# Block products in a mixture-of-experts kernel: reordering the engines' queues, loading w_out a group earlier, and feeding the sums between half-steps

## The chip, the cores and the metric

One core of one Trainium2 chip. The metric is the device time of one execution in microseconds (us), the median over runs. The profile shows one execution. TensorE is called PE here, its weight loads PEld, VectorE DVE, ScalarE ACT, GpSimd POOL, and SyncE, which issues most DMAs, SP. Every engine works through its own queue in the order in which the built program has it.

## The reference

Three stages run one after the other on 2304 tokens of 512 values: random-feature attention, a gated feed-forward layer, and a layer of 8 experts with room for 288 tokens each.

```
x = attention(q, k, v, omega)                   # [2304, 512]
xn = x / rms(x) * rms_g
h = silu(xn @ w_gate) * (xn @ w_val)            # [2304, 1536]
y = h @ w_out
logits = y @ moe2_w_gate                        # [2304, 8]; greedy assignment, highest logit first
out[mask_e] = relu(y[mask_e] @ w1[e]) @ w2[e]   # for each expert e
```

The change touches only how `h` and the sums for it are scheduled, and the end of the attention stage before it.

## The kernel before, in words

Every float32 product is made of three products of a rounded "high" part and a "low" remainder, so each operand appears twice: a high copy (on ACT) and a low difference (on DVE or POOL). A product of two 128-row steps is therefore six matmuls (`product`).

The tokens form five blocks of 512, 512, 256, 512 and 512 columns. **Attention** runs in 81 ticks (`run_tick`), one item of work each, with up to five older items still in flight. Into these ticks go *half-steps* of the feed-forward layer for the first three blocks (`ffn_step_pe` and `ffn_step_el`: one half of `h` for 128 of the 1536 features, gate or value, twelve matmuls, then tanh on ACT, two products on DVE, the split of `h`, and its write to DRAM, `h_dr`), and *units* (`conv_pe`, `conv_el`), which unscramble 48 pieces of weights from 64-bit words: one ACT operation and three DVE operations each (lines 591 to 593). `PACE` is the number of units started per tick, `STEP` the number of half-steps per tick.

The last two blocks, LEFT and RIGHT, are not multiplied one by one. They are treated as one 2 by 2 block product that is done with seven products instead of eight (Winograd's form of Strassen). For this the **sums stage** forms four sums of x (`sum_1` to `sum_4`, from the sum `sum_left` of the high and low parts of LEFT, and a split copy of half of RIGHT, `r2`), each in two column halves. While DVE, ACT and POOL do that, PE finishes the half-steps of the small 256-column block that are left over.

Then come twelve **groups** (`group(f)`, f from 0 to 11, and a short thirteenth), one for each 128 features. In the program's order PE does in a group: the product `pa` (in bank gv), a `late` logit (below), the product `pe` (also a gv bank), the logits of LEFT of the group before, a product added to bank `bb`, one added to `pa`, the logits of RIGHT, a product added to `bb`, one to `bc`, one to `bd`. Between them stand: `copy(bb, pa)` and `copy(p5, pe)` on ACT; `bc = bb + p5` on DVE, which has to be done before PE may add to `bb` again; `copy(bd, bb)` on ACT; the gates (`gate` is tanh on ACT, `times_gate` and `times_value` are DVE), and the split of h (`keep_high` on ACT, `keep_low` on DVE with the DMA to `h_dr`). A group also prepares work for others: `turn_w(f, part)` makes the sums of the weights (part 0 on POOL two groups ahead, parts 1 and 2 on DVE, parts 3 and 4 the split into `ta` on ACT and POOL); `wo_split` loads two 128-row pieces of w_out, makes the high copy on ACT and leaves the low parts to `wo_part` on DVE; `lates_lg` and `lates_split` load, split, write back and multiply with the gate weights the twelve pieces of h of the first block ("late", tile xh on ACT and POOL); `ffn_rank_el` compares logits of two 128-token chunks per call (`ranks`, part on DVE, part on `st["eng"]`).

In the groups PE, DVE, ACT and POOL keep the written order (`manual_schedule`); in the sums stage and in attention only PE does, and a scheduler places the rest. After the groups, w_out's product (`ffn2`, 648 matmuls) is used as filler while DVE sorts the tokens to the experts (`route`), and the experts follow.

Of the kernel before, what the change touches and what calls it, by code (L numbers as in the profile page):

```python
# [51 lines left out]
STEP = 1.08  # L52
PACE = (0.5, 0.7, 0.65)
# [241 lines left out]
def kernel(ctx, tc, qT, kT, kC, v1, vC, om, wgv, rms, wo, woT, wg2, w1, w2, cfd, trd, out, dbg=None):  # L295
# [443 lines left out]
    st["eng"] = st["sub"] = nc.gpsimd  # L739
    st["rank"] = lambda: psL.tile([128, BLK // 128, 2 * E], F32, name="lg")  # L740

    def ffn_rank_el():
        for c0 in rks:
            ranks(nc, st["eng"], fp, cf[:, C_T:C_N].rearrange("p (a b) -> p a b", b=E), L, R, c0, 2)
        rks.clear()

    def ffn_step_pe():
        if not ready or ready[0][1:] not in gvs or (fq and fq[0][1] not in wogs):
            return False
        j, f, v = ready.pop(0)  # L750
        pg = ffn_pe(j, f, v)
        if (f, v) == (KF - 1, 1):
            del xblk[j]
        ffn_rank()
        if v and fq:
            ffn_lg(*fq.pop(0))
        fst["el"] = (j, f, v, pg)
        return True
# [78 lines left out]
    def run_tick(tick):  # L837
# [6 lines left out]
        ffn_step_pe()  # L844
# [17 lines left out]
        if tick >= FFN_AT:  # L862
            conv["step"] += STEP - 1
            if conv["step"] >= 1:
                conv["step"] -= 1
                ffn_step_pe()
                ffn_step_el()
# [27 lines left out]
    def wo_part():  # L895
# [17 lines left out]
    st["late"] = 0  # L913
# [8 lines left out]
    def late_split(f):  # L922
        hs = lates[f]
        nc.scalar.copy(hs[:, :, 0], hs.bitcast(F32)[:, :, 1])
        nc.gpsimd.tensor_sub(hs[:, :, 1], hs.bitcast(F32)[:, :, 1], hs[:, :, 0])  # L925
        nc.sync.dma_start(h_dr[:BLK // HB2, :, f].rearrange("b p x -> p b x"),
                          hs.bitcast(F32).rearrange("p b l t -> p b (l t)"))

# [5 lines left out]
    def sum_tile(name):  # L934
        pool, kw = (xp, dict(name="xl")) if name == "s3" else (sp, dict(name=name))
        t = pool.tile([128, 2, 2, BLK], F32R, **kw)
        sums[name] = t
        return t

    def sum_split(name, half, t, eng):  # L940
        s_ = slice(half * HF, half * HF + HF)
        o = sums[name] if name in sums else sum_tile(name)
        nc.scalar.copy(o[:, 0, :, s_], t)
        eng.tensor_sub(o[:, 1, :, s_], t, o[:, 0, :, s_])

    lf = {}

    def sum_left(half):
        s_ = slice(half * HF, half * HF + HF)
        lf[half] = stage.tile([128, KD, HF], F32, name="ws")  # L950
        nc.vector.tensor_add(lf[half], xlh[:, :, s_], xll[:, :, s_])
# [4 lines left out]
    s1, s2 = {}, {}  # L956

    def sum_1(half):
        s_ = slice(half * HF, half * HF + HF)
        s1[half] = temp()  # L960
        nc.vector.tensor_add(s1[half], xr[:, :2, s_], xr[:, 2:, s_])
        sum_split("s1", half, s1[half], nc.vector)

    def sum_2(half):
        nc.vector.tensor_sub(s1[half], s1[half], lf[half][:, :2])
        sum_split("s2", half, s1[half], nc.vector)

    def sum_3(half):
        s_ = slice(half * HF, half * HF + HF)
        t = temp()  # L970
        nc.vector.tensor_sub(t, lf[half][:, :2], xr[:, :2, s_])
        sum_split("s3", half, t, nc.gpsimd)

    def sum_4(half):
        nc.vector.tensor_sub(s1[half], lf[half][:, 2:], s1[half])
        sum_split("s4", half, s1[half], nc.vector)
        s_ = slice(half * HF, half * HF + HF)
        sum_split("r2", half, xr[:, 2:, s_], nc.gpsimd)

    def turn_w(f, part):  # L980

        b, t = wf.get(f), wf.get(("t", f))
        if part == 0:
            w = wsl[f]
            wf[f] = stage.tile([128, 4, HF], F32, name="ws")
            for h in (slice(0, 2), slice(2, 4)):
                nc.gpsimd.tensor_add(wf[f][:, h], w[:, 0].rearrange("p (b x) -> p b x", b=4)[:, h],  # L987
                                     w[:, 1].rearrange("p (b x) -> p b x", b=4)[:, h])
# [6 lines left out]
        else:  # L995
            i = part - 3
            o = ta[f, i] = sp.tile([128, 2, 2, HF], F32R, name="ta", bufs=3)
            nc.scalar.copy(o[:, 0], t[i])  # L998
            nc.gpsimd.tensor_sub(o[:, 1], t[i], o[:, 0])  # L999
# [42 lines left out]
    def group(f):  # L1042

        nxt = f + 1 if f + 1 < KF else None
        if f < KF:
# [11 lines left out]
        if f < KF:  # L1057
# [6 lines left out]
        if f < KF:  # L1064
            pe = wide(psG, "gv")
            product(pe, *t1, *both("s1"), True)
        if f:
            keep_low(RIGHT, f - 1, th2, hp2)
        if f == KF:
            return  # L1070
        p5 = wide(sp, "p5", bufs=2)
        nc.scalar.copy(p5, pe)
        if nxt:
            turn_w(nxt, 1)
            turn_w(nxt, 3)
# [16 lines left out]
        nc.scalar.copy(bd, bb)  # L1092
        nc.vector.tensor_add(p5, bb, p5)
        if nxt:
            turn_w(nxt, 4)
        if f + 2 < KF:
            turn_w(f + 2, 0)
        product(bc_, *b22, *both("s4"), False)
        ffn_rank()
        st["rank"] = lambda: psS.tile([128, 512], F32, name="late")[:, :BLK // 128 * 2 * E].rearrange(  # L1100
            "p (c e) -> p c e", e=2 * E)
# [14 lines left out]
    def lates_lg():  # L1116
        n = st["late"]
        if 0 < n <= KF:
            ffn_lg(0, n - 1, lates[n - 1])
            if n == KF:  # L1120
                st["late"] += 1
        if 0 < n < KF - 1:
            late_load(n + 1)

    def lates_split():
        if st["late"] < KF:
            late_split(st["late"])
            st["late"] += 1

    with tc.manual_schedule(engines={mybir.EngineType.PE}):  # L1130
        ins = iter([lambda: sum_left(0), lambda: sum_1(0), lambda: sum_1(1), lambda: sum_left(1),
                    lambda: turn_w(0, 0), lambda: sum_2(0), lambda: sum_2(1), lambda: sum_3(0), lambda: sum_3(1),
                    lambda: sum_4(0), lambda: sum_4(1), lambda: turn_w(0, 1), lambda: turn_w(0, 2),
                    lambda: turn_w(0, 3), lambda: turn_w(0, 4), lambda: turn_w(1, 0)])
        while ready:
            assert ffn_step_pe()
            ffn_step_el()
            for _ in range(2):
                next(ins, int)()
        for make in ins:  # L1140
            make()
        late_load(0)
        late_load(1)
        while fq:
            ffn_lg(*fq.pop(0))
        for t in (bb, bc_, bd):
            nc.tensor.matmul(t, xlh[:, 0, :128], xlh[:, 0], start=True, stop=True)
    with tc.manual_schedule(engines=in_order | {mybir.EngineType.Pool}):
# [332 lines left out]
```

## Time and profile before

| what | us |
|---|---|
| median of 3 runs (lowest, highest) | 935.31 (934.28, 936.63) |
| the profiled execution's own time | 935.55 |
| its span, first to last instruction | 933.8 |
| PE busy in the span | 887.0 (95%) |
| attention with half-steps and units, up to | 334 |
| sums stage | 334 to 361 |
| first matmul of groups 0, 1, 2, 3 | 361.00, 372.47, 386.27, 397.23 |
| first matmul of the w_out product, after the groups | 518.81 |

The span and the 1.75 us around it make the time of the profiled execution. Busy time of PE counts overlapping matmuls as modelled, so that the time between the starts of two matmuls is the better measure of its pace.

### The profile page before, as it was taken

The numbers are of one execution on the slowest core, as the hardware profiler recorded it, in microseconds if no ns is written. First come the engines' busy times: TensorE is split into PE (matmuls) and PEld (weight loads), VectorE is DVE, ScalarE is ACT, GpSimd is POOL, SyncE is SP. The second block draws the span as 40 slices with busy tenths as digits, with TensorE's granted clock in tenths as the row PEclk, the third lists the DMA queues.
The fourth block names the chain that finished last, engine by engine and source line by source line (L and its number), as shares of the span: only waits on it lengthen the run. The fifth ranks groups of instructions, "written<-read, shape, count | busy, mean of one in ns | idle before, by whom it ended". The sixth has DMA issues, their size and how long they took to land.

```text
span 933.8 us, 15697 instructions
## 1 busy us (share of the span) xinstructions
PE 887.0 (95%) x5780; PEld 764.2 (82%) x5780; DVE 624.8 (67%) x1392; ACT 412.3 (44%) x913; POOL 264.1 (28%) x317
## 2 busy tenths in 40 slices
PE   9999999999999978988889899999999999999996
PEld 8788888888889976656657677777779999999996
DVE  4899876566659996665677667777664655566652
ACT  5886665445446643444444201001004544454541
POOL 1364423223323366555543000000011222222211
PEclk9999999999999999999999999999999999999999
DMA  8656436443355424554535987777732566755651
GB/s 289 203 152 205 148 101 181 134 144 113 128 180 188 148 77 127 190 193 158 188 119 188 247 229 206 226 208 212 210 94 86 180 193 194 215 183 187 190 178 32
DMA packets 114110, 159.26 MB, mean 171 GB/s; under 512 B 6641, under 2 KB 71665, under 8 KB 114033
## 3 DMA queue, kind: packets, MB, share of 16 engines
q1 hardware_dynamic: 108224, 143.96, 49.7%
q0 software_dynamic: 3072, 9.44, 3.5%
q10 hardware_dynamic: 2736, 4.85, 1.4%
q8 instruction: 45, 0.74, 0.3%
q14 instruction: 33, 0.26, 0.1%
HBM read 114.19 MB, written 44.04 MB: 169 GB/s over the span
## 4 chain that ended last, share of the span: by engine, by line
PE 39%; issue 10%; DVE 10%; POOL 5%; ACT 2%; DMA 2%; SPq 0%; POOLq 0%; ACTq 0%; DVEq 0%
PE py L1225 15%; PE ph L1337 3%; PE ph L1340 3%; PE ph L1338 3%; PE py L1350 3%; PE py L1348 3%; PE py L1349 3%; DVE hp L1025 1%; DMA ws<-wo_dr 1%; POOL ws L987 1%; POOL xh L925 1%; POOL ta L999 1%; POOL out_dram L1384 1%; PE gv L1320 1%; PE po L1354 1%
## 5 line engine op out<-in xcount | busy, mean ns | idle before, releaser
L1225 PE MATMUL py<-wc,ht 128*128 128x512 f32 x624 | 160.2, 405 | 0.4 <-DMA ht<-h_dr 0.4
L1225 PEld LDWEIGHTS py<-wc,ht 128*128 128x128 f32 x624 | 112.6, 191 | 20.1 <-DMA ht<-h_dr 0.5
L675 PE MATMUL gv<-xh,wc 128*128 128x512 f32 (+1 forms) x288 | 105.5, 377 | 4.5 <-DVE th L688 3.3
L1196 DVE TENSOR_TENSOR wc<-ws,wc 128x512 fp32r<-128x512 f32 x128 | 84.6, 685 | 35.5 <-ACT wc L1206 35.5
L676 PE MATMUL gv<-xh,wc 128*128 128x512 f32 (+1 forms) x288 | 100.0, 358 | 0.0
L408 ACT ACTIVATE ft<-pp,mx 128x128 f32<-128x128 f32 x288 | 83.0, 375 | 27.6 <-DVE mx L405 27.2
L1350 PE MATMUL py<-ehh,wc 128*128 128x288 f32 x256 | 76.2, 298 | 0.0
L1348 PE MATMUL py<-ehh,wc 128*128 128x288 f32 x256 | 75.8, 296 | 0.0
L1349 PE MATMUL py<-ehl,wc 128*128 128x288 f32 x256 | 75.6, 295 | 0.0
L1337 PE MATMUL ph<-exh,wc 128*128 128x288 f32 x256 | 71.2, 300 | 0.0
L1236 ACT COPY ys<-py 128x512 f32<-128x512 f32 x18 | 10.6, 588 | 134.8 <-PE py L1225 126.9
L1338 PE MATMUL ph<-exh,wc 128*128 128x288 f32 x256 | 69.8, 296 | 0.0
L1206 ACT CAST wc<-ws 128x1024 fp32r<-128x1024 f32 x64 | 67.3, 1052 | 2.7 <-ACT ys L1236 2.7
L678 PE MATMUL gv<-xl,wc 128*128 128x512 f32 (+1 forms) x288 | 67.5, 356 | 0.0
L675 PEld LDWEIGHTS gv<-xh,wc 128*128 128x128 f32 x288 | 54.7, 190 | 12.6 <-DVE th L688 4.6
L1342 DVE SCALAR_TENSOR_TENSOR ehl<-ph,ehh 128x288 fp32r<-128x288 f32 x64 | 29.3, 458 | 46.6 <-ACT ehh L1341 43.2
L676 PEld LDWEIGHTS gv<-xh,wc 128*128 128x128 f32 x288 | 54.9, 191 | 6.5
L405 DVE TENSOR_REDUCE mx<-pp 128x4 f32<-128x512 f32 (+1 forms) x76 | 50.0, 658 | 15.1 <-PE pp L401 9.1
L678 PEld LDWEIGHTS gv<-xl,wc 128*128 128x128 f32 x288 | 49.7, 191 | 8.2
L1276 POOL DMA_INDIRECT xh<-y_dr,idc x3 | 3.1, 1040 | 171.4 <-DVE idc L1288 170.8
L999 POOL TENSOR_TENSOR ta<-dw,ta 128x512 fp32r<-128x512 f32 x24 | 31.6, 1318 | 66.6 <-ACT ta L998 66.4
L1384 POOL DMA_INDIRECT out_dram<-yo,ids x24 | 22.5, 939 | 98.1 <-DVE yo L1379 75.3
(305 smaller groups left out, 2218.1 us busy)
## 6 DMA issues: line engine op xcount, KB each, us to landing
ws<-in_w_dram SPq DMA_DIRECT2D x64, 512.0 KB, 4.1
ht<-h_dr SPq DMA_DIRECT2D x53, 512.0 KB, 4.4
h_dr<-hp SPq DMA_DIRECT2D x36, 512.0 KB, 3.0
ws<-in_wgv_dram SPq DMA_DIRECT2D x24, 512.0 KB, 4.7
h_dr<-hp SPq DMA_DIRECT2D x24, 256.0 KB, 3.1
ws<-in_woT_dram SPq DMA_DIRECT2D x12, 512.0 KB, 3.5
ws<-in_wo_dram SPq DMA_DIRECT2D x12, 512.0 KB, 3.6
h_dr<-xh SPq DMA_DIRECT2D x12, 512.0 KB, 2.9
```

Source lines behind the costliest of these rows:

```text
L408: st["ex"] = nc.scalar.activation(ft[:n, g], pp[:n, g], AF.Exp, bias=mx[:n, g:g + 1])
L675: nc.tensor.matmul(pg[:, :n], w[:, 0, v, k], xh[:, k, :n], start=(k == 0), stop=False)
L676: nc.tensor.matmul(pg[:, :n], w[:, 1, v, k], xh[:, k, :n], start=False, stop=False)
L678: nc.tensor.matmul(pg[:, :n], w[:, 0, v, k], xl[:, k, :n], start=False, stop=(k == KD - 1))
L1196: nc.vector.tensor_sub(w[:, 1, h], sv[:, h], w[:, 0, h])
L1206: nc.scalar.copy(w[:, 0], sv)
L1225: nc.tensor.matmul(py, ht[:, i4, a], w[:, l, f % 2], start=(f == 0 and n == 0), stop=(f == KF - 1 and n == 2))
L1337: nc.tensor.matmul(ph, w[:, 0, k, m], xh[:, k], start=(k == 0), stop=False)
L1338: nc.tensor.matmul(ph, w[:, 1, k, m], xh[:, k], start=False, stop=False)
L1348: nc.tensor.matmul(py, w[:, 0, k], hh[:, k], start=(k == 0), stop=False)
L1349: nc.tensor.matmul(py, w[:, 0, k], hl[:, k], start=False, stop=False)
L1350: nc.tensor.matmul(py, w[:, 1, k], hh[:, k], start=False, stop=(k == KE - 1))
```

## The change

**The groups.** `wo_split` becomes `wo_load` (the DMA, in odd groups), and `wo_high` (the ACT copy) with two `wo_low` (DVE), which take place in the next even and the next odd group. `turn_w` part 0 is cut into two halves (0 and 5) and moves from behind `turn_w(nxt, 4)` to behind `times_gate(th1)`; parts 3 and 4 become `turn_high` (ACT) and `turn_low` (POOL). `late_split` moves to the head of the group and, in odd groups, to the middle. Rank comparisons come one call per group, on DVE instead of POOL.

**The sums stage.** All four engines keep the written order. The sums are a list of 16 entries, and one entry is issued after each half-step; the last low parts move into group 0.

**Attention.** From tick 71 on, only half a half-step per tick is issued instead of 1.08, and `PACE` of the last third is 0.75 instead of 0.65. As the tables work out, 16 half-steps instead of 10 are left for the sums stage, and all units have started by tick 72 instead of 77.

**After the groups** the first fillers are 8, 3, 6 and 3 matmuls with the ranks between them, instead of 9, 10 and 5 with the ranks behind.

```diff
-STEP = 1.08
-PACE = (0.5, 0.7, 0.65)
+STEP = (1.08, 0.5)
+SLOW_AT = 71
+PACE = (0.5, 0.7, 0.75)
...
-        ffn_step_pe()
+        rate = STEP[0] if tick < SLOW_AT else STEP[1]
+        conv["step"] += rate if tick >= FFN_AT else 0
+        if conv["step"] >= 1:
+            conv["step"] -= ffn_step_pe()
...
-    def wo_split(c):
+    def wo_load(c):
         sv = stage.tile([128, 2, DM], F32, name="ws")
         nc.sync.dma_start(sv, wo_dr[2 * c:2 * c + 2].rearrange("f p d -> p f d"))
-        w = wpool.tile([128, 2, 1024], F32R, name="wc")
-        sv = sv.rearrange("p f d -> p (f d)")
+        st["wo"] = sv.rearrange("p f d -> p (f d)")
+
+    def wo_high():
+        sv, w = st["wo"], wpool.tile([128, 2, 1024], F32R, name="wc")
         nc.scalar.copy(w[:, 0], sv)
         wos.append(w)
         parts.extend((w, sv, slice(h, h + 512)) for h in (0, 512))
...
+    def late_split():
+        if late["split"] < len(lates):
+            late_high(late["split"])
+            late_low(late["split"])
+            late["split"] += 1
+
+    def late_lg():
+        f = late["lg"]
+        if f < late["split"]:
+            ffn_lg(0, f, lates[f])
+            late["lg"] += 1
+            if f + 2 < KF:
+                late_load(f + 2)
...
+        late_lg()
+        if not f:
+            sum_low("s4", 1, s1[1], nc.vector)
+            sum_low("r2", 1, right_2(1), nc.gpsimd)
+            late_load(0)
+            late_load(1)
         if f:
+            keep_low(LEFT, f - 1, *old["l"])
             th2 = wide(fp, "th")
             gate(th2, bd)
-            keep_low(LEFT, f - 1, *old["l"])
             times_gate(th2, bd)
-        if f < KF:
+            times_value(th2, old["p5"])
+            late_split()
+        if not last:
             nc.scalar.copy(bb, pa)
         if f:
             hp2 = pair()
-            times_value(th2, old["p5"])
             keep_high(th2, hp2)
-        lates_lg()
+        if nxt:
+            turn_w(nxt, 1)
...
         product(bb, *t2, *both("s2"), False)
         if nxt:
             turn_w(nxt, 2)
-        lates_split()
+            turn_high(nxt, 0)
+            turn_low(nxt, 0)
         nc.vector.tensor_add(bc_, bb, p5)
+        if f % 2:
+            wo_low()
+            wo_load(f // 2)
         product(pa, *b21, *a12, False)
-        wo_part()
         th1 = wide(fp, "th")
         gate(th1, pa)
         times_gate(th1, pa)
+        if f + 2 < KF:
+            turn_w(f + 2, 0)
+            turn_w(f + 2, 5)
         logits_of(RIGHT)
+        if f % 2 and f > 1:
+            late_lg()
+            late_split()
         product(bb, *t3, *both("s3"), False)
-        if f % 2:
-            lates_lg()
-            lates_split()
+        if f and not f % 2:
+            wo_high()
+            wo_low()
...
         times_value(th1, bc_)
-        ffn_rank_el()
-        wo_part()
-        if f > 1 and not f % 2:
-            wo_split(f // 2 - 1)
         keep_high(th1, hp1)
+        ffn_rank_el(1)
...
+    ins = [[lambda: sum_left(0)],
+           [lambda: sum_1(0)],
+           [lambda: sum_3(0), lambda: sum_low("s1", 0, s1[0], dve)],
+           [lambda: sum_left(1), lambda: sum_low("s3", 0, s3[0], pool)],
...
+    with tc.manual_schedule(engines=in_order | {mybir.EngineType.Pool}):
+        count, rounds = len(ready), len(ins)
         while ready:
+            el = fst.pop("el", None)
             assert ffn_step_pe()
-            ffn_step_el()
-            for _ in range(2):
-                next(ins, int)()
...
+            if el:
+                ffn_el(*el)
+                ffn_rank_el()
+            while len(ins) > rounds * len(ready) // count:
+                for make in ins.pop(0):
+                    make()
```

ACT's queue in group 2, the first one with a copy of w_out, from the gate on `bd` to the next group's gate: of before, and then of the change (tile p_... is p5, tile xh the late split, wc the copy of w_out, hp the high part of h).

```order
L1032 ACTIVATE th<-bd 128x512
L1058 COPY bb<-gv 128x512
L1022 CAST hp<-th 128x2x256
L1072 COPY p_4537<-gv 128x512
L998 CAST ta<-dw 128x512
L924 CAST xh<-xh 128x2x256
L1032 ACTIVATE th<-gv 128x512
L1092 COPY bd<-bb 128x512
L998 CAST ta<-dw 128x512
L891 CAST wc<-ws 128x1024
L1022 CAST hp<-th 128x2x256
L1032 ACTIVATE th<-bd 128x512
```

```order
L1055 ACTIVATE th<-bd 128x512
L928 CAST xh<-xh 128x2x256
L1089 COPY bb<-gv 128x512
L1045 CAST hp<-th 128x2x256
L1102 COPY p_4535<-gv 128x512
L1019 CAST ta<-dw 128x512
L1055 ACTIVATE th<-gv 128x512
L896 CAST wc<-ws 128x1024
L1128 COPY bd<-bb 128x512
L1019 CAST ta<-dw 128x512
L1045 CAST hp<-th 128x2x256
L1055 ACTIVATE th<-bd 128x512
```

The copy of w_out moved from the place right ahead of the high part of h and the next gate to one ahead of `copy(bd, bb)`, and the late split moved to the head of the group.

DVE's queue at the head of the sums stage: of before, and then of the change (dw<-ws,dw on lines 592 and 593, or 593 and 594, belongs to the units; s_... are the sums' tiles, ws the sum of LEFT).

```order
L592 SCALAR_TENSOR_TENSOR dw<-ws,dw 128x512
L961 TENSOR_TENSOR dw<-xh 128x512
L593 SCALAR_TENSOR_TENSOR dw<-ws,dw 128x512
L688 SCALAR_TENSOR_TENSOR th<-th,gv 128x256
L961 TENSOR_TENSOR dw<-xh 128x512
L944 TENSOR_TENSOR s_4095<-dw,s_4095 128x2x256
L699 SCALAR_TENSOR_TENSOR th<-gv,th 128x256
L944 TENSOR_TENSOR s_4095<-dw,s_4095 128x2x256
L951 TENSOR_TENSOR ws<-xh,xl 128x1024
L688 SCALAR_TENSOR_TENSOR th<-th,gv 128x256
```

```order
L594 SCALAR_TENSOR_TENSOR dw<-ws,dw 128x512
L551 SCALAR_TENSOR_TENSOR xn<-x,ss,gr 128x512
L700 SCALAR_TENSOR_TENSOR th<-gv,th 128x256
L975 TENSOR_TENSOR ws<-xh,xl 128x512 x2
L689 SCALAR_TENSOR_TENSOR th<-th,gv 128x256
L982 TENSOR_TENSOR dw<-xh 128x512
L700 SCALAR_TENSOR_TENSOR th<-gv,th 128x256
L991 TENSOR_TENSOR dw<-ws,xh 128x512
L970 TENSOR_TENSOR s_4004<-dw,s_4004 128x2x256
L689 SCALAR_TENSOR_TENSOR th<-th,gv 128x256
```

Between two operations of the half-steps (th) there are now one or two of the sums. The first sum of LEFT (L975, now in two pieces) stands in the stage; before, the scheduler had placed it in the attention's tail, and the L951 shown is the sum for the second column half.

SP's queue around the second load of w_out: of the change (ws<-wo_dr is the load, h_dr<-hp the writes of h by `keep_low`, xh<-h_dr and h_dr<-xh the load and the write-back of a late piece).

```order
L923 DMA xh<-h_dr 128x2x256
L933 DMA h_dr<-xh 128x2x512
L1050 DMA h_dr<-hp 128x2x512
L891 DMA ws<-wo_dr 128x2x512
L1050 DMA h_dr<-hp 128x2x512
L923 DMA xh<-h_dr 128x2x256
L933 DMA h_dr<-xh 128x2x512
```

The load stands between the write of RIGHT of one group and the write of LEFT of the next, about two groups ahead of its copy; before, it stood behind the late write-back of the same even group.

## Rows read from the trace of the kernel before

**Rows 1.** Stretches: length, busy PE, PEld, DVE, ACT, POOL, clock, DMA.

```profile
280.00:297.60 17.60, 17.60 (x125) 16.00 (x124) 16.29 (x40) 10.40 (x28) 5.74 (x6) 1.00 0.64 202
297.60:334.00 36.40, 35.59 (x295) 33.85 (x294) 32.94 (x79) 24.77 (x67) 15.05 (x24) 1.00 0.40 133
334.00:361.00 27.00, 17.60 (x131) 15.29 (x131) 26.91 (x31) 9.37 (x20) 21.09 (x15) 1.00 0.27 90
372.47:517.34 144.87, 127.76 (x535) 92.70 (x533) 95.66 (x139) 66.98 (x117) 71.84 (x59) 0.99 0.49 168
530.00:690.00 160.00, 158.09 (x1139) 118.80 (x1138) 115.36 (x435) 16.11 (x23) 0.00 (x0) 0.99 0.73 210
```

**Rows 2.** Timeline of PE: start us, us, instruction, idle before and releaser.

```profile
372.47 0.39 PE L1004 MATMUL gv<-xh,wc 128*128 128x512 f32 x1
...
386.27 0.39 PE L1004 MATMUL gv<-xh,wc 128*128 128x512 f32 x1
...
397.23 0.39 PE L1004 MATMUL gv<-xh,wc 128*128 128x512 f32 x1
...
419.97 0.50 PE L1004 MATMUL bb<-xl,ta 128*128 128x512 f32 x1 [0.85 <-DVE bc L1081]
...
429.75 0.41 PE L720 MATMUL lg<-hp,wog 128*16 128x512 f32 x1 [2.19 <-ACT hp L1022]
...
518.81 0.50 PE L1225 MATMUL py<-wc,xh 128*128 128x512 f32 x1 [1.47 <-DVE th L1035]
```

**Rows 3.** Waits of PE, 362 to 514 us: total us, times, longest.

```profile
PE bb L1004 <- DVE bc L1081: 8.2, 8, 1.2
PE lg L721 <- DVE hp L1025: 4.5, 5, 3.0
PE lg L720 <- ACT hp L1022: 3.4, 3, 2.2
```

**Rows 4.** Waits of ACT, 362 to 518 us.

```profile
ACT wc L891 <- DMA ws<-wo_dr: 12.8, 3, 5.4
```

**Rows 5.** Timeline of ACT at the end of group 4.

```profile
428.13 1.05 ACT L891 CAST wc<-ws 128x1024 fp32r<-128x1024 f32 x1 [5.37 <-DMA ws<-wo_dr]
429.09 0.61 ACT L1022 CAST hp<-th 128x512 fp32r<-128x512 f32 x1
```

**Rows 6.** Timeline of SP: the issue of that load.

```profile
422.13 0.46 SPq L888 DMA_DIRECT2D ws<-wo_dr  x1
```

**Rows 7.** Timeline of DVE, end of group 3 and group 4.

```profile
407.84 0.67 DVE L1035 SCALAR_TENSOR_TENSOR th<-th,gv 128x512 f32<-128x512 f32 x1
...
413.30 1.78 DVE L1025 TENSOR_TENSOR hp<-th,hp 128x512 fp32r<-128x512 f32 x1
...
417.09 0.69 DVE L1025 TENSOR_TENSOR hp<-th,hp 128x512 fp32r<-128x512 f32 x1 [0.69 <-ACT hp L1022]
...
419.22 0.69 DVE L1081 TENSOR_TENSOR bc<-bb,p 128x512 f32<-128x512 f32 x1
```

**Rows 8.** Timeline of POOL in the same stretch.

```profile
407.33 2.99 POOL L925 TENSOR_TENSOR xh<-xh 128x512 fp32r<-128x512 f32 x2
...
411.54 2.99 POOL L987 TENSOR_TENSOR ws<-wc 128x512 f32<-128x512 f32 x2
...
419.12 1.31 POOL L999 TENSOR_TENSOR ta<-dw,ta 128x512 fp32r<-128x512 f32 x1 [4.59 <-ACT ta L998]
```

**Rows 9.** Groups of DVE, 297 to 361 us, by shape: count, busy, mean ns.

```profile
L593 DVE SCALAR_TENSOR_TENSOR dw<-ws,dw 128x512 int32<-128x512 int32 x6 | 5.3, 882 | 0.0
L592 DVE SCALAR_TENSOR_TENSOR dw<-ws,dw 128x512 int32<-128x512 int32 x6 | 5.1, 856 | 0.0
```

**Rows 10.** Timeline of PE: start of a half-step and the matmul behind it.

```profile
341.92 0.28 PE L675 MATMUL gv<-xh,wc 128*128 128x256 f32 x1
...
343.36 0.28 PE L720 MATMUL lg<-hp,wog 128*16 128x256 f32 x1
```

**Rows 11.** DMA issues: count, KB each, median us to landing.

```profile
xh<-h_dr SPq DMA_DIRECT2D x12, 256.0 KB, 2.8
```

More of the change, by code (lines that the diff above doesn't have):

```diff
@@ L739, with ffn_rank_el @@
     st["eng"] = st["sub"] = nc.gpsimd
+    st["behind"] = False
     st["rank"] = lambda: psL.tile([128, BLK // 128, 2 * E], F32, name="lg")
-    def ffn_rank_el():
-        for c0 in rks:
+    def ffn_rank_el(most=NC):
+        for c0 in rks[:most]:
             ranks(nc, st["eng"], fp, cf[:, C_T:C_N].rearrange("p (a b) -> p a b", b=E), L, R, c0, 2)
-        rks.clear()
+        del rks[:most]
     def ffn_step_pe():
@@ L754, in ffn_step_pe @@
         ffn_rank()
-        if v and fq:
+        if len(fq) > 1 if st["behind"] else v and fq:
             ffn_lg(*fq.pop(0))
@@ L861, in run_tick @@
             items[tick + AHEAD].load()
[L862 to L866, printed above, removed]
-                ffn_step_el()
+        while conv["step"] >= 1:
+            conv["step"] -= 1
+            ffn_step_pe()
+            ffn_step_el()
     with tc.manual_schedule(engines={mybir.EngineType.PE}):
@@ L927, in late_split @@
                           hs.bitcast(F32).rearrange("p b l t -> p b (l t)"))
+    late = dict(split=0, lg=0)
+    def late_split():
[10 more added lines that the diff above has]
+                late_load(f + 2)
     HF = BLK // 2
@@ L932, with half_of @@
     wf, ta, sums = {}, {}, {}
[L934 to L943, printed above, removed]
+    lf, s1, s3 = {}, {}, {}
+    def half_of(half):
+        return slice(half * HF, half * HF + HF)
@@ L944, in sum_split, with sum_high, sum_low @@
+    def sum_high(name, half, t):
+        if name not in sums:
+            pool, kw = (xp, dict(name="xl")) if name == "s3" else (sp, dict(name=name))
+            sums[name] = pool.tile([128, 2, 2, BLK], F32R, **kw)
+        nc.scalar.copy(sums[name][:, 0, :, half_of(half)], t)
+    def sum_low(name, half, t, eng):
+        o, s_ = sums[name], half_of(half)
         eng.tensor_sub(o[:, 1, :, s_], t, o[:, 0, :, s_])
-    lf = {}
     def sum_left(half):
-        s_ = slice(half * HF, half * HF + HF)
@@ L974, in sum_4, with right_2 @@
+        sum_high("s3", half, s3[half])
     def sum_4(half):
         nc.vector.tensor_sub(s1[half], lf[half][:, 2:], s1[half])
-        sum_split("s4", half, s1[half], nc.vector)
-        s_ = slice(half * HF, half * HF + HF)
-        sum_split("r2", half, xr[:, 2:, s_], nc.gpsimd)
+    def right_2(half):
+        return xr[:, 2:, half_of(half)]
     def turn_w(f, part):
         b, t = wf.get(f), wf.get(("t", f))
-        if part == 0:
+        if part in (0, 5):
             w = wsl[f]
[L985 to L988, printed above, removed]
+            if part == 0:
+                wf[f] = stage.tile([128, 4, HF], F32, name="ws")
+            h = slice(2 * (part > 0), 2 * (part > 0) + 2)
+            nc.gpsimd.tensor_add(wf[f][:, h], w[:, 0].rearrange("p (b x) -> p b x", b=4)[:, h],
+                                 w[:, 1].rearrange("p (b x) -> p b x", b=4)[:, h])
@@ L994, in turn_w, with turn_high, turn_low @@
             nc.vector.tensor_sub(t[1][:, 1], b[:, 1], t[1][:, 0])
[L995 to L999, printed above, removed]
+    def turn_high(f, i):
+        ta[f, i] = sp.tile([128, 2, 2, HF], F32R, name="ta", bufs=3)
+        nc.scalar.copy(ta[f, i][:, 0], wf["t", f][i])
+    def turn_low(f, i):
+        nc.gpsimd.tensor_sub(ta[f, i][:, 1], wf["t", f][i], ta[f, i][:, 0])
     def product(bank, wh, wl, xh, xl, start):
@@ L1114, in logits_of @@
             ffn_lg(*fq.pop(0))
[L1116 to L1134, printed above, removed]
+    dve, pool = nc.vector, nc.gpsimd
@@ L1153 @@
                 ffn2_load(*seq2[1], x2, "xl2", 1)
-    wo_split(KF // 2 - 1)
-    while parts:
-        wo_part()
+        wo_high()
+        wo_low()
+        wo_low()
     ss.close()
@@ L1251, in fill @@
         return True
-    with tc.manual_schedule(engines={mybir.EngineType.PE}):
-        for n in (9, 10):
+    with tc.manual_schedule(engines=in_order):
+        for n in (8, 6):
             fill(n * FILL_MM)
             ffn_lg(*fq.pop(0))
-        fill(5 * FILL_MM)
-        ffn_rank()
-    ffn_rank_el()
+            fill(3 * FILL_MM)
+            ffn_rank()
+            ffn_rank_el()
     if "L" in dbg:
```

73 lines of the change are left out of this document (40 added, 33 removed).

## The prediction

> **What bounds the kernel now.** I read the stretches first [rows 1], because PE's 95% over the whole span is a mean over stages with different limits. From 530 to 690 us PE is busy for 158.1 of 160 us, so nothing that is only moved there can matter. In the groups, 372.47 to 517.34 us, no engine is full: PE shows 127.8 of 144.9 us, DVE 95.7, POOL 71.8, ACT 67.0. In the sums stage, 334 to 361 us, DVE is full (26.9 of 27.0) and PE is not (17.6). In the 36 us ahead of it PE is nearly full (35.6 of 36.4) and so is DVE (32.9).
>
> Next, the pace that PE could have in the groups. Group 2 goes from 386.27 to 397.23 [rows 2] with 48 matmuls (seven products of six, three logits of two), none of which waits: 10.96 us, 0.2283 us each. From the first matmul of group 1, 372.47, to the end of the products, 518.81 - 1.47 = 517.34 [rows 2], the program has 11 groups of 46 matmuls and 24 for the late logits, 530, so 121.0 us at that pace. It takes 144.87. **The excess is 23.9 us**, all of it waits and the slow restart behind each.
>
> Who is waited for: DVE's `bc` add, 8.2 us in 8 waits of 0.85 to 1.2; the halves of LEFT's h for the logits, 4.5 and 3.4 us [rows 3]. Two chains stand behind them.
>
> The first is the copy of w_out. In even groups ACT reaches it before its load has landed, 12.8 us in three waits [rows 4]. In group 4 the load is issued at 422.13 [rows 6], the copy begins at 428.13 after 5.37 us of idle ACT, and only behind it come the high part of h and the gates [rows 5]; PE stands 2.19 us for that high part at 429.75 [rows 2].
>
> The second is DVE beside POOL. The low part of h takes 0.69 us at 417.09, but 1.78 us at 413.30 [rows 7], where POOL makes the sums of weights, 411.54 to 414.53 [rows 8]. The gate at 407.84, which reads one input from PSUM, takes 0.67 us [rows 7] inside POOL's 407.33 to 410.32 [rows 8]. So a DVE operation with both inputs in SBUF waits for POOL's current one, and others do not. The 1.1 us lost at 413.30, and as much lost ahead of it, are still there when the `bc` add starts at 419.22 [rows 7], and PE waits for it until 419.97 [rows 2].
>
> **The change, part by part.**
>
> *w_out a group ahead.* The load now stands in SP's queue between RIGHT's write of one group and LEFT's of the next, so it is issued about two groups, over 20 us, before its copy; landing took 6.0 us in the case above. ACT's 12.8 us go. On PE I charge this chain with 7.5 us: 3.4 for the high part, about 1.3 of the 4.5 for low parts that came right behind it, and 2.8 for the restarts and for the work of the next products that was late with it. Queued behind SP's load are h writes, which nobody waits for within a group.
>
> *The sums of weights.* POOL's two operations (1.3 to 1.5 us each) move from the group's end, where `keep_low` and `wo_low` ran into them, to the middle, where DVE's next steps are the gate on `pa` and the sum into p5, both with an input in PSUM. What can collide there is `wo_low`, and it has slack. At the group's head POOL now has the late split (1.3 us), which can catch `times_value(th2)`. By durations from the rows, with time from the group's first matmul: tanh on `bd` ends at 0.8, `times_gate` at 1.5, `times_value` is held until the late split ends at 2.65 and is done at 3.2, against 4.3 in group 4 before. Then one weight sum (0.7), RIGHT's low part (0.7), two half weight sums (0.9), the last of which can meet POOL's split of `ta` (1.3): `bc` is done between 6.0 and 7.2. PE asks for it after 30 matmuls, at 6.85. So its wait of about 1 us becomes 0 to 0.35, and I keep 0.2 with 0.3 for the restart in each of 11 groups: 5.4 us of the excess stay.
>
> *Ranks.* One wait of 3.0 us [rows 3] belongs to the late block's comparisons, two calls in one group with trips to POOL. One call per group on DVE alone removes it; the two added DVE operations per call are hidden where DVE waits for `bc`'s product. Without that cover they cost under 1 us in two groups.
>
> So the groups lose 23.9 - 5.4 = 18.5 us. The bounds are 10 (the copy's chain and the ranks alone) and 23.
>
> *Sums stage and attention's tail* belong together, since half-steps only move from one to the other. From 297.6 to 361 us PE is idle for 63.4 - 53.2 = 10.2 us [rows 1], which no reordering can exceed. DVE is the limit at the end of it. Between tick 71 and the first group its queue holds three units fewer, each two operations of 0.87 us [rows 9] and a shorter one that I estimate at half of that: 3 x 2.2 = 6.5 us. But two of the three go into the ticks just ahead, where DVE is busy for 16.3 of 17.6 us [rows 1]. The sums themselves are the same operations. In the written order DVE spends rounds of two half-steps with three or four sums each, longer than PE's 1.44 us per half-step (341.92 to 343.36 [rows 10]) in the first ten rounds, and little in the last six. I take a gain of **4 us**. Lower bound: if all 16 half-steps went at the old stage's 27.0 / 10 = 2.7 us, the stage would take 43.2 instead of 27.0 and the tail save 6 x 1.44 = 8.6, a loss of 7.6. Upper bound: 10.
>
> *Zero:* group 0 (its new wait is DVE's `bc` behind the small block's ranks, which PE's 30 matmuls cover; about 1 us if not); the first fillers, 20 instead of 24 matmuls, since PE works through the same 648 (0.9 us if DVE's sorting were the limit, but PE is [rows 1]); POOL's sums for group 0, now ahead of the tail's norm operations (up to 2 us, inside the 4 above).
>
> **Sum.** 933.8 - 18.5 - 4 = 911.3 us of span, with 1.75 us around it **913 us** against 935.55 of the profiled execution; that stood 0.24 above the median, which does not matter here.
>
> **A rule weighed against the rows.** By the rows above, a two-input DVE operation loses what is left of one POOL operation. The Trainium skill, in SBUF — State Buffer, section SBUF: two separate sides, calls the port pair of the two an exclusive lock, held for the whole instruction by who starts first. The trace agrees: 1.78 us against 0.69, and 0.67 for the operation with a PSUM input. By that rule moving POOL's work gains nothing by itself; it only chooses who is held. Its own result is the first rival.
>
> **Rivals.**
>
> *The collision moves and the `bc` waits stay.* POOL has 5 operations of 1.3 us in an even group and 6 in an odd one with a late piece, DVE about 4.3 us with two SBUF inputs; 10.8 and 12.1 us together, against 11 to 11.4 of PE. For it: the late split now falls into the chain to `bc`. Against: with that counted, the chain came out 1 us earlier. If the waits stay at 8.2 us plus restarts of 2.5, the groups gain 18.5 - 5.3 = 13 us, and the time is 918 to 919. Chance 0.22.
>
> *The sums stage eats a part.* In order, PE's next half-step waits for a gv bank that DVE frees behind the sums. At the pace of 2.7 us the 7.6 us above are lost: 935.55 - 18.5 + 7.6, 924 to 925. For it: DVE is full there now. Against: six rounds have hardly a sum. Chance 0.08.
>
> *Slower: ACT waits for late pieces as it did for w_out.* In odd groups a late piece is loaded behind the logit at the group's head (2 us) and copied on ACT after the gate on `pa`, at about 7 us. The load lands 2.8 us after issue [rows 11], so there are 2 us to spare. The old loads waited on SP behind late write-backs. If each of the 11 copies stood for the 3.9 us or so by which a w_out copy delayed its group, 43 us would be lost for 22.5 gained: 955. It decides against the change from a mean wait of about 2 us per copy, that is, from loads 4 us later than now. Chance 0.03.
>
> *Nothing moves:* the lock binds the groups at 12.1 to 12.5 us and the sums stage loses its 7.6 us; 931 to 936. Chance 0.04.
>
> **Chances.** The forecast, 907 to 917, has 0.60; better than that, with nearly all waits gone, 0.03. Within 0.3% is about what a measurement here can tell from no change, 2.8 us. Faster 0.92, same 0.03, slower 0.05. The range from 904 to 922 leaves out the last three rivals and little of the first: it should hold with the bounds of the groups (10 to 23) at a gain of 4 elsewhere.
>
> **What the profile would show.** Right: no wait of ACT for ws<-wo_dr; group starts 11 to 11.8 us apart from group 2 on, with no even-odd pattern; PE's waits for `bc` below 4 us in sum; from 297 us to group 0 about 4 us less. Wrong: waits of ACT's late copy for its DMA; `bc` waits near 1 us with POOL's `ta` or late split beside DVE's weight sums; half-steps more than 2.5 us apart over the whole stage. The point most likely to be off is the residual 0.5 us per group, which is worked out from durations and not seen.

## The result, and the profile after

The changed kernel takes **908.51 us** (median of 4 runs, 907.23 to 912.01) against 935.13 of the kernel before beside it: a ratio of 0.972, 95% interval 0.9689 to 0.975. 913 was forecast, with a range of 904 to 922. Its profiled execution took 909.13 us, with a span of 907.3.

Three stages share the 26.5 us of span between the two profiled executions: 3.2 up to the first matmul of group 1 (372.47 [rows 2], now 369.28), 19.1 in groups 1 to 11 (144.87 [rows 1], now 125.76), and 4.2 from the first matmul of w_out's product to the end (933.8 - 518.81, now 907.3 - 496.51). Stretches of the changed kernel: the tail of attention and the sums stage, group 0, groups 1 to 11, the first 22.7 us behind them (columns as in [rows 1]).

```profile
297.60:354.04 56.44, 51.94 (x421) 48.64 (x419) 45.74 (x101) 31.65 (x82) 30.71 (x38) 1.00 0.21 77
354.04:369.28 15.24, 14.02 (x51) 10.59 (x50) 6.30 (x11) 4.40 (x10) 8.37 (x8) 0.78 0.57 173
369.28:495.04 125.76, 123.56 (x535) 92.45 (x533) 107.84 (x139) 66.88 (x117) 67.00 (x52) 1.00 0.55 194
495.04:517.70 22.66, 20.36 (x132) 14.93 (x132) 17.82 (x55) 5.35 (x10) 1.21 (x4) 1.00 1.03 278
```

Group 0 starts 6.96 us earlier (361.00 before, 354.04 now) but takes 15.24 us instead of 11.47, at a clock of 0.78. PE's waits in the changed kernel, 297 to 370 and 369 to 496 us:

```profile
PE lg L722 <- POOL hp L710: 2.7, 2, 1.5
...
PE bb L1027 <- DVE bc L1109: 2.2, 6, 0.7
```

The second row is all that PE's list has for the groups, where [rows 3] had 16.1 us; ACT's list has no row for w_out's load any more [rows 4]. PE's timeline, joint and groups:

```profile
353.91 0.29 PE L722 MATMUL lg<-hp,wog 128*16 128x256 f32 x1 [1.50 <-POOL hp L710]
354.04 0.39 PE L1027 MATMUL gv<-xh,wc 128*128 128x512 f32 x1
...
356.46 0.39 PE L722 MATMUL lg<-hp,wog 128*16 128x256 f32 x1 [1.22 <-POOL hp L710]
...
359.83 0.63 PE L1028 MATMUL gv<-s,ta 128*128 128x512 f32 x1
360.26 0.63 PE L1027 MATMUL gv<-s,ta 128*128 128x512 f32 x1
...
403.65 0.39 PE L1027 MATMUL gv<-xh,wc 128*128 128x512 f32 x1
...
410.92 0.50 PE L1027 MATMUL bb<-xl,ta 128*128 128x512 f32 x1 [0.30 <-DVE bc L1109]
...
415.14 0.39 PE L1027 MATMUL gv<-xh,wc 128*128 128x512 f32 x1
...
426.62 0.39 PE L1027 MATMUL gv<-xh,wc 128*128 128x512 f32 x1
```

Groups start 11.45 to 11.49 us apart from group 1 to 9; group 9 takes 12.03 and group 10 11.30. At the joint, where the sums stage ends and group 0 begins, logits of the small block stand among the first matmuls of group 0 and wait for POOL's low parts; behind that a matmul takes 0.63 us and the next starts 0.43 later, where it is 0.39 and 0.23 elsewhere: the lower of the two clock levels. In the kernel before such a logit stood there too, but waited 0.21 us. What is new is POOL's lateness: it splits group 0's half of r2 ahead of the last low part. PE before, then POOL in the changed kernel:

```profile
362.78 0.30 PE L721 MATMUL lg<-hp,wog 128*16 128x256 f32 x1 [0.21 <-POOL hp L709]
```

```profile
353.82 1.73 POOL L970 TENSOR_TENSOR r<-xh,r 128x512 fp32r<-128x512 f32 x1
355.50 0.91 POOL L710 TENSOR_TENSOR hp<-th,hp 128x256 fp32r<-128x256 f32 x1
```

What is left in the groups shows on DVE, by shape (count, busy, mean ns, idle time ahead):

```profile
L1048 DVE TENSOR_TENSOR hp<-th,hp 128x512 fp32r<-128x512 f32 x23 | 17.2, 746 | 8.6 <-ACT hp L1045 7.6
L1015 DVE TENSOR_TENSOR dw<-ws,dw 128x256 f32<-128x256 f32 x10 | 15.6, 1556 | 0.3
L1061 DVE SCALAR_TENSOR_TENSOR th<-p,th 128x512 f32<-128x512 f32 x11 | 15.4, 1397 | 0.4
...
L1061 DVE SCALAR_TENSOR_TENSOR th<-bc,th 128x512 f32<-128x512 f32 x11 | 7.6, 692 | 1.3 <-PE bc L1030 0.5
```

`th<-p` has both inputs in SBUF and takes 1397 ns on the mean, `th<-bc` reads PSUM and takes 692.

### The profile page after: what moved, and what is told of

It reads as the page before. It is cut to its first block, busy times and chain, and to the rows that moved or that the text cites. A ratio compares the mean times of both kernels' runs of the same rounds, so it can differ in the third digit from the quotient of the medians.

```text
span 907.3 us, 15714 instructions
## 1 busy us (share of the span) xinstructions
PE 881.3 (97%) x5780; PEld 763.0 (84%) x5780; DVE 633.5 (70%) x1398; ACT 412.3 (45%) x913; POOL 259.3 (29%) x313
## 4 chain that ended last, share of the span: by engine, by line
PE 46%; issue 8%; DVE 6%; POOL 3%; ACT 1%; DMA 0%; POOLq 0%; ACTq 0%; DVEq 0%
PE py L1264 15%; PE ph L1376 3%; PE ph L1379 3%; PE ph L1377 3%; PE py L1389 3%; PE py L1387 3%; PE py L1388 3%; DVE th L1061 1%; PE bb L1027 1%; PE gv L1030 1%; PE gv L1028 1%; PE gv L1027 1%; PE bb L1028 1%; PE bb L1030 1%; POOL out_dram L1423 1%
## 5 line engine op out<-in xcount | busy, mean ns | idle before, releaser
L676 PEld LDWEIGHTS gv<-xh,wc 128*128 128x128 f32 x288 | 54.5, 189 | 10.5 <-DVE th L689 2.4
L1423 POOL DMA_INDIRECT out_dram<-yo,ids x24 | 22.5, 938 | 98.1 <-DVE yo L1418 75.4
L1380 ACT ACTIVATE ehh<-ph 128x288 fp32r<-128x288 f32 x64 | 26.4, 412 | 49.7 <-PE ph L1379 49.7
```

The lines of the kernel that those rows point to most:

```text
L676: nc.tensor.matmul(pg[:, :n], w[:, 0, v, k], xh[:, k, :n], start=(k == 0), stop=False)
```

## The experiments

**Theory:** two chains made the groups slow, the late copy of w_out (7.5 us) and POOL's sums of weights in DVE's way; half-steps between the sums gave the gain ahead of them; waits and the clock behind them made the joint slow and, in the kernel before, the start of w_out's product. **Rivals** stand in each expectation. The times come from several chips, each with the kernel before beside it, so the ratio compares them. The profiled executions split as follows (us; with 1.47 between the second and third they make the span):

| kernel | median | ratio | to group 1 | groups 1 to 11 | behind |
|---|---|---|---|---|---|
| before | 935.1 | 1 | 372.47 | 144.87 | 414.99 |
| changed | 908.51 | 0.972 | 369.28 | 125.76 | 410.79 |
| w_old | 911.0 | 0.9752 | 369.08 | 127.11 | 410.74 |
| w_place | 909.65 | 0.9728 | 371.98 | 125.51 | 410.74 |
| sums_end | 919.44 | 0.9841 | 367.83 | 136.43 | 410.87 |
| late_mid | 908.94 | 0.9718 | 371.42 | 123.49 | 410.72 |
| rank_pool | 910.38 | 0.9745 | 368.83 | 127.83 | 410.77 |
| steps_old | 915.45 | 0.9798 | 375.94 | 125.44 | 410.85 |
| fill_old | 912.35 | 0.9762 | 369.76 | 125.65 | 414.92 |
| joint | 904.82 | 0.969 | 363.42 | 125.94 | 410.77 |
| b_load | 924.96 | 0.9887 | 372.67 | 134.35 | 415.01 |
| b_sums | 921.32 | 0.9855 | 370.08 | 131.49 | 415.46 |
| joint_swap | 900.54 | 0.9629 | 364.12 | 121.89 | 410.82 |
| joint_late_swap | 901.41 | 0.9638 | 365.43 | 122.74 | 410.86 |

The interval of the changed kernel's ratio reaches 3 us to either side, those of the others 1.2 to 2.3, so differences of 1 to 3 us are read from the stage that an edit touches. Each stage is read from one execution. The time to group 1 scatters most: the seven kernels whose code is that of the changed one up to group 0 (it, w_old to rank_pool, and fill_old) start group 0 between 354.03 and 356.70.

**The chain of w_out undone in the changed kernel: w_old.**

```diff
         if f % 2:
             wo_low()
-            wo_load(f // 2)
...
         if f and not f % 2:
-            wo_high()
             wo_low()
...
         times_value(th1, bc_)
+        if f > 1 and not f % 2:
+            wo_load(f // 2 - 1)
+            wo_high()
...
```

> The changed kernel with the load and the high copy of w_out back at the end of the even group, as before the change; the low parts stay where the change has them. The prediction charged the chain of the w_out copy with 7.5 us: by it ACT waits for the load again, about 5 us a time, PE waits for the high part of h, and the time goes from 908.5 to 915 to 917 us. Rival: with the other edits in place DVE and ACT have the slack to take the late copy, ACT's waits come back but PE's do not: 908.5 to 910.5 us.

The groups take 1.4 us more. ACT waits for the load again, four times but 2.5 us in all; PE's list has bc alone:

```profile
ACT wc L896 <- DMA ws<-wo_dr: 2.5, 4, 1.1
...
PE bb L1027 <- DVE bc L1109: 2.6, 7, 0.7
```

911.0 us is just above the rival's range and far below the theory's: undone alone, this part is worth little. But the load did not become as late as it was. Group 4 of w_old, PE and SP:

```profile
403.79 0.39 PE L1027 MATMUL gv<-xh,wc 128*128 128x512 f32 x1
...
406.54 0.36 SPq L933 DMA_DIRECT2D h_dr<-xh  x1
...
410.40 0.36 SPq L891 DMA_DIRECT2D ws<-wo_dr  x1
```

The load is issued 6.61 us behind the group's first matmul; in the kernel before it was 9.99 (412.14 to 422.13). There it stood behind the write-back of a late piece; here that write-back went out early, since the late split is at the group's head. So 1.4 us is not the price of the old lateness.

**Its place alone: w_place** (the load as changed, `wo_high()` where w_old has it).

> The changed kernel with the load of w_out still a group ahead, but the high copy (1.05 us of ACT) back at the end of the even group, in front of the high part of h. If the lead of the load is what counts, no ACT wait for the load is seen and the time stays within 1.5 us of 908.5. Rival: the place counts, the copy holds the high part of h and the next gate by 1.05 us in each of 5 groups, and the time is 912 to 914 us.

125.51 us in the groups, and no wait of ACT for the load: the place costs nothing, as the theory had it. The 2.7 us more ahead of group 1 are not the edit's (last section).

**POOL's sums of weights back at the group's end: sums_end.**

```diff
-        if f + 2 < KF:
-            turn_w(f + 2, 0)
-            turn_w(f + 2, 5)
         logits_of(RIGHT)
...
             turn_low(nxt, 1)
+        if f + 2 < KF:
+            turn_w(f + 2, 0)
+            turn_w(f + 2, 5)
         ffn_rank()
```

> The changed kernel with the two POOL sums of weights for the group after next back at the end of the group, behind the last split of ta. If the collision of these with DVE's low parts was what made DVE late, the low part of h at the group's end takes 1.8 instead of 0.7 us again, PE's waits for bc come back at 0.5 to 1 us per group, and the time is 914 to 918 us. Rival: the collision only changes who is held, the chain to bc stays inside PE's 6.85 us, and the time is 908 to 910.5 us.

10.7 us more in the groups, the most that any undone part costs; 919.44 us is above the 914 to 918 of the theory. ACT has no wait for w_out here, so this is the sums' place alone. PE's waits for bc are back, and the low part of h takes 1016 instead of 746 ns on the mean:

```profile
PE bb L1027 <- DVE bc L1109: 10.8, 10, 1.6
...
L1048 DVE TENSOR_TENSOR hp<-th,hp 128x512 fp32r<-128x512 f32 x23 | 23.4, 1016 | 7.8 <-ACT hp L1045 7.6
L1061 DVE SCALAR_TENSOR_TENSOR th<-p,th 128x512 f32<-128x512 f32 x11 | 11.0, 1003 | 0.4
```

**The late split back in the middle: late_mid.**

```diff
             times_value(th2, old["p5"])
-            late_split()
...
             turn_low(nxt, 0)
+        if f:
+            late_split()
         nc.vector.tensor_add(bc_, bb, p5)
```

> The changed kernel with the late split of the group's head back in the middle, ahead of the bc add; the second one of odd groups stays. The prediction has times_value at the head held by the late split, with the chain to bc still 1 us shorter than before: in the middle POOL's split collides with the second sum of weights on DVE and with the bc add itself, bc waits grow to about 0.5 us per group, and the time is 911 to 914 us. Rival: the head was the worse place, times_value is free now, and the time is 905 to 908 us.

The rival is nearer, though 908.94 us lies in neither range: the groups take 2.3 us less, and `times_value` at the head is free, 692 instead of 1397 ns. The last sum of weights is shorter as well, 880 instead of 1556 ns, so the 2.3 us are not those of `times_value` alone:

```profile
L1061 DVE SCALAR_TENSOR_TENSOR th<-p,th 128x512 f32<-128x512 f32 x11 | 7.6, 692 | 0.4
L1015 DVE TENSOR_TENSOR dw<-ws,dw 128x256 f32<-128x256 f32 x10 | 8.8, 880 | 0.3
```

The time is the changed kernel's, since this execution lost 2.1 us ahead of group 1, where nothing was edited.

**Ranks on POOL, all of a block in one group: rank_pool.** `st["eng"] = nc.vector` ahead of the groups is left out, and `ffn_rank_el(1)` becomes `ffn_rank_el()`.

> The changed kernel with the rank comparisons on POOL for the subtractions and all calls of a block in one group, as before the change. The prediction has one wait of 3.0 us of PE for a low part of h behind these: 911 to 912 us. Rival: with the rest of the order changed the trips to POOL are hidden, and the time is 908 to 909.5 us.

2.1 us more in the groups, between the two: PE waits 0.9 us for h, not 3.0, and group 10 takes 13.4 instead of 11.3 us. The 3.0 us of before were not the ranks' alone. There the first comparison (L91) met POOL's sums of weights; in b_sums (below), which moves these sums and leaves the ranks on POOL, it did not, and PE waited 0.94 us in place of 3.00. The kernel before, then b_sums:

```profile
479.10 2.60 POOL L987 TENSOR_TENSOR ws<-wc 128x512 f32<-128x512 f32 x2
479.29 1.25 DVE L91 TENSOR_TENSOR rk_g<-L 128x128 f32<-128x128 f32 x1
```

```profile
466.58 0.28 DVE L91 TENSOR_TENSOR rk_g<-L 128x128 f32<-128x128 f32 x1
...
471.12 0.41 PE L721 MATMUL lg<-hp,wog 128*16 128x512 f32 x1 [0.94 <-DVE hp L1025]
```

**Half-steps as before: steps_old.**

```diff
-STEP = (1.08, 0.5)
+STEP = (1.08, 1.08)
-PACE = (0.5, 0.7, 0.75)
+PACE = (0.5, 0.7, 0.65)
```

> The changed kernel with 1.08 half-steps per tick to the end and 0.65 units, as before: 10 half-steps are left for the sums stage instead of 16, all else as changed. If the gain ahead of the groups comes from PE having work between the sums, group 0 starts 4 to 8 us later and the time is 912 to 916 us. Rival: the written order of the sums alone made it, and the time is 907.5 to 910 us.

Group 0 starts at 360.67, where it stood before the change (361.00): the written order of the sums alone gave 0.3 us, and what this run undoes, the half-steps kept back and the pace of the units, the other 6.6 (4.0 against the latest of the kernels that have both, 356.70). Which of these two it was no run tells apart.

**Fillers and ranks as before: fill_old.**

```diff
-        for n in (8, 6):
+        for n in (9, 10):
             fill(n * FILL_MM)
             ffn_lg(*fq.pop(0))
-            fill(3 * FILL_MM)
-            ffn_rank()
-            ffn_rank_el()
+        fill(5 * FILL_MM)
+        ffn_rank()
+    ffn_rank_el()
```

> The changed kernel with the first fillers and ranks after the groups as before (9, 10 and 5 matmuls, ranks behind). The changed kernel gained 4.2 us there, which the prediction had at nothing. If that came from the clock, which fell to 0.92 over 517 to 540 us in the kernel before and stays at 1.00 now, the old fillers cost under 1 us: 908 to 909.5 us. Rival: the order of fillers and ranks made it, by PE's waits for the sorting that start earlier: 911 to 913 us.

The rival holds: 414.92 us behind the groups, as in the kernel before (414.99); in the table all kernels with the new fillers have 410.7 to 410.9 there, and all with the old ones 414.9 to 415.5. With the ranks behind all fillers DVE's sorting starts later, PE waits for it, and then runs at the lower clock; fillers and ranks were undone together, not each alone. The stretch of the same length as the fourth row of the changed kernel, PE's wait in fill_old, and the same wait in the changed kernel:

```profile
495.41:518.07 22.66, 18.71 (x94) 13.80 (x93) 15.25 (x47) 5.36 (x10) 1.17 (x4) 0.92 1.02 275
...
PE cnt L188 <- DVE xh L142: 2.5, 1, 2.5
...
PE cnt L188 <- DVE xh L142: 0.8, 1, 0.8
```

The clock's fall went with the fillers; it did not move to group 0.

**The joint in one written order: joint.** The small block's rest and the groups stand in one `manual_schedule`, with the last logits inside group 0 and POOL's split of r2 behind the last low part:

```diff
-        while fq:
-            ffn_lg(*fq.pop(0))
-        ffn_rank()
-        ffn_rank_el()
...
         product(pe, *t1, *both("s1"), True)
+        while not f and fq:
+            ffn_lg(*fq.pop(0))
```

> The changed kernel with the rest of the small block and the groups in one written order: the last two logits of the small block stand behind the second product of group 0, its ranks behind the fourth, and POOL's last split of r2 behind the last low part of h. In the changed kernel PE waits 1.5 and 1.22 us for low parts of h at the joint and then runs at half clock for about 6 us; group 0 takes 15.2 us instead of the 11.5 of before. If the waits are what brings the clock down, both go and 3.5 to 5 us with them: 903.5 to 905.5 us, with a granted clock of 1.00 from 353 to 370 us. Rival: the clock falls anyway, there or in a later stretch (in the kernel before it fell at the start of the w_out product), and only the waits are gained: 906 to 908 us.

Group 0 takes 10.44 us at full clock, and group 1 starts 5.9 us earlier; of the time 5.7 us show between the two profiled executions (909.13 and 903.40), 3.7 between the medians, 2.8 by the ratios, whose intervals overlap. The stage is clear, though: the three kernels with this joint take 10.44 us for group 0, the eight others with the written order of the sums 13.8 to 15.3. What the waits cost and what the clock does is not told apart, since both went.

```profile
352.98:363.42 10.44, 10.44 (x49) 8.31 (x48) 7.10 (x11) 4.33 (x10) 8.70 (x7) 1.00 0.81 246
```

**The same two parts from the other side: b_load and b_sums.** One edit each in the kernel before: the load in odd groups with the copy at its old place, and `turn_w(f + 2, 0)` behind `times_gate(th1, pa)`.

> The kernel before with one edit: w_out is loaded a group ahead, in odd groups, and the copy on ACT stays where it was. The prediction charged the chain of that copy with 7.5 us of the 24 us that the groups lose: by it 927 to 929 us. Rival: undoing it in the changed kernel cost only 2.5 us, so that it is worth 2 to 3 us from this side too, 932 to 933.5 us, and the rest of the 7.5 was the collision's.

> The kernel before with one edit: POOL's sums of weights for the group after next, in one piece as before, behind the gate on pa instead of at the group's end. Undoing this in the changed kernel cost 11 us. If the two causes are apart, it is worth the same from this side, 923 to 926 us. Rival: the late copy of w_out and the late split still make DVE late and hide a part, 928 to 932 us.

Both times, 924.96 and 921.32 us, are below both of their ranges. The groups gain 10.5 and 13.4 us, more than the prediction's share for the one and more than undoing showed for both. Together that would be 23.9, and the change as a whole gives 19.1, so the two do not add up. One reason is that PE's waits for bc, 8.2 us before [rows 3], fall with the load alone (first row, b_load); another, that b_sums moved more than POOL's sums (the other rows):

```profile
PE bb L1006 <- DVE bc L1083: 4.2, 4, 1.2
...
ACT wc L891 <- DMA ws<-wo_dr: 3.1, 3, 2.0
...
PE bb L1004 <- DVE bc L1081: 5.1, 6, 1.2
```

ACT's waits for w_out fell from 12.8 to 3.1 us, though the load was not edited. The first matmul of group 4 and SP's timeline, of b_sums and of the kernel before:

```profile
406.48 0.39 PE L1004 MATMUL gv<-xh,wc 128*128 128x512 f32 x1
...
412.57 0.46 SPq L888 DMA_DIRECT2D ws<-wo_dr  x1
416.06 0.36 SPq L926 DMA_DIRECT2D h_dr<-xh  x1
```

```profile
412.14 0.39 PE L1004 MATMUL gv<-xh,wc 128*128 128x512 f32 x1
...
421.72 0.36 SPq L926 DMA_DIRECT2D h_dr<-xh  x1
```

In the kernel before the load is issued behind that write-back, at 422.13 [rows 6], and the write-back waits for POOL's split of the late piece. SP has no written order, and with the sums moved the scheduler put the load ahead of it. The write-back itself stands 9.58 us behind the group's first matmul in both kernels, so POOL's sums did not hold it: b_sums moved the load in SP's queue, and its 13.4 us cannot be the sums' alone. Their own price, in the changed kernel, is that of sums_end, 10.7.

**What is left in the groups: joint_swap and joint_late_swap.**

```diff
-        if f:
-            keep_low(RIGHT, f - 1, th2, hp2)
...
         if nxt:
             turn_w(nxt, 2)
+        if f:
+            keep_low(RIGHT, f - 1, th2, hp2)
+        if nxt:
             turn_high(nxt, 0)
```

> The kernel with the joint in one written order (904.8 us) with one more edit: in the groups the second and third difference of weights on DVE stand ahead of the low part of RIGHT's h instead of behind it. In the changed kernel the last of these differences takes 1.56 us instead of 0.42 in even groups, since POOL's split of ta runs beside it, and bc is 0.3 us late. Ahead of the low part they start before that split. If this is the rest of the excess in the groups (4.8 us), the bc waits go and the time is 901 to 903 us. Rival: the low part of h is held instead, for as long, and nothing changes: 904 to 905.5 us.

The edit is made in joint. It takes **900.54 us** (900.11 to 900.66; ratio 0.9629, interval 0.9616 to 0.9643), the fastest here. PE has no wait in the groups, and L1015 went from 1556 to 426 ns, while `times_value` at the head is still held:

```profile
364.12:486.01 121.89, 121.89 (x535) 93.14 (x533) 94.33 (x140) 66.41 (x117) 69.77 (x54) 1.00 0.58 200
...
L1015 DVE TENSOR_TENSOR dw<-ws,dw 128x256 f32<-128x256 f32 x10 | 4.3, 426 | 0.3
L1061 DVE SCALAR_TENSOR_TENSOR th<-p,th 128x512 f32<-128x512 f32 x11 | 14.4, 1312 | 0.4
```

> The same with the late split of the group's head moved to the middle as well, so that times_value at the head takes 0.69 instead of 1.35 us. With the chain to bc already short enough nothing is left to gain, within 0.7 us of the run without it. Rival: the split collides in the middle with the low part of h or the bc add's inputs, and the time is 1 to 3 us more; or the group starts 10.96 us apart in even groups only here, 1 to 2 us less.

901.41 us, 0.9 more in the groups, between the 0.7 expected and the rival's 1 to 3. The two intervals overlap (0.9625 to 0.9651 here); no gain is left.

## Why the prediction was right, and where its steps were not

In all 22.5 us were forecast and 26.5 measured in the span; the 4 us more are those of the first fillers, and the rest came out in sum, not step by step.

*The groups:* 18.5 us forecast, 19.1 measured. The pace of 0.2283 us per matmul held: joint_swap needs 121.89 us where 121.0 was worked out. The residue was 125.76 - 121.0 = 4.8 us for 5.4 forecast (its 0.5 us in 11 groups make 5.5), and most of it, 4.05 us between joint and joint_swap, came from the place that the working named last: the sum of weights that meets POOL's split of `ta` (1556 ns, gone with joint_swap). The prediction had the late split at the head as the main collision; that one was there too, but late_mid, which shortened L1015 as well, took out 2.3 us only, and with L1015 free it costs nothing (joint_late_swap).

*The price of the two chains* was wrong as a split. 7.5 us for w_out's copy is too little for its worth alone (10.5): the prediction put the waits for bc to POOL's collisions, and half of them, 4.0 of 8.2 us, went with the load. That the old loads stood behind late write-backs it says only among its rivals; so it did not see that the late split's new place frees the load too (w_old), nor that SP's order can change with the sums (b_sums). How far the parts overlap stays open.

*Collisions.* The Trainium skill, in SBUF — State Buffer, section SBUF: two separate sides, has a DVE operation with two SBUF inputs and one of POOL take a port pair in turn, for a whole instruction. The pairs of rows agree: 692 against 1397 ns, 426 against 1556. "Moving POOL's work gains nothing by itself" does not hold: undoing the move of the sums cost 10.7 us (sums_end). "It only chooses who is held" does, and who is held decides the price: held for 1312 ns on the mean in joint_swap, `times_value` cost nothing, and L1015, held for 1556, cost 4.05 us.

*Ranks:* 3.0 forecast as one wait, 2.1 measured undone. Of that wait 2.06 us went with POOL's sums of weights as well (0.94 in b_sums), so it did not belong to the comparisons alone.

*Sums stage and tail:* 4 us forecast, 3.2 measured up to group 1, right by luck: two errors cancelled. Half-steps and units gave 6.6, the order of the sums 0.3, and **group 0, charged with nothing, lost 3.8**: the working looked at bc and not at the small block's last logits, which the scheduler set among the first product and which wait for POOL.

*The first fillers, charged with nothing,* gave 4.1 us (fill_old). "PE works through the same 648" left out that PE stands once for the sorting and is slow behind it: with the old fillers the wait is 2.48 us instead of 0.79, and with the slow stretch behind it and four matmuls more ahead of it that made over 4.

*Rivals.* The bc waits did not stay (2.2 of 8.2), no late copy held ACT, the sums stage was not slower. (The sum of the third gives 956, not 955.)

## What to carry to other kernels

Before giving two waits a price each, follow each late transfer back through its queue. Undo and do each part alone, and then read the queues of each built program: a one-line edit can move a transfer that it does not name, and undoing an edit need not bring back what it cured. Where two written orders meet, read the built order at the seam, for what a scheduler interleaves there belongs to neither. Price a wait of PE together with the slow stretch that may follow it.

## What was not expected of the hardware

The lower clock follows some waits and not others. In the changed kernel 1.50 and 1.22 us at the joint brought it. In the kernel before, the 2.19 us in group 5 [rows 2] did, and the longest wait of the groups, 3.00 us at 485.88, did not; that wait, and the stretches of group 5 and of group 9, which has it:

```profile
485.88 0.41 PE L721 MATMUL lg<-hp,wog 128*16 128x512 f32 x1 [3.00 <-DVE hp L1025]
...
424.18:440.52 16.34, 13.46 (x51) 9.33 (x50) 8.27 (x13) 7.45 (x13) 8.57 (x8) 0.90 0.47 162
479.75:494.94 15.19, 10.96 (x48) 8.11 (x46) 11.33 (x19) 5.21 (x10) 6.39 (x9) 1.00 0.29 104
```

Even the same wait did both: at 205 us PE waits 1.24 us for a half-step in w_place and 1.23 in the changed kernel. PE's timeline of w_place, then of the changed kernel:

```profile
205.36 0.80 PE L676 MATMUL gv<-xh,wc 128*128 128x512 f32 x1 [1.24 <-DVE th L689]
205.96 0.63 PE L677 MATMUL gv<-xh,wc 128*128 128x512 f32 x1
206.38 0.63 PE L676 MATMUL gv<-xh,wc 128*128 128x512 f32 x1
```

```profile
204.22 0.50 PE L676 MATMUL gv<-xh,wc 128*128 128x512 f32 x1 [1.23 <-DVE th L689]
204.56 0.39 PE L677 MATMUL gv<-xh,wc 128*128 128x512 f32 x1
204.79 0.40 PE L676 MATMUL gv<-xh,wc 128*128 128x512 f32 x1
```

This accounts for 1.5 of the 2.7 us by which w_place reaches group 1 later; the start of group 0 differs by as much, 2.7 us, among the seven kernels with the same code up to there. At the joint, too, the same waits (2.7 us in two) left group 0 at a clock of 0.88 and 13.8 us in three of the seven, and at 0.78 and 15.2 to 15.3 us in four. What decides whether the clock falls stays open.
